# Issuing part of the loads and swaps of a fused attention and feed-forward kernel from GpSimd, and copying w_out in pairs

## The chip, the core and the metric

The kernel runs on one core of a Trainium2 chip. The metric is the device time of one execution in microseconds (us). The core has TensorE (PE; its weight loads are listed as PEld), VectorE (DVE), ScalarE (ACT), GpSimd (POOL) and SyncE (SP), each with an instruction queue of its own that is worked off in order. Data move by DMA on 16 DMA engines; a DMA is an instruction in the queue of the engine that issues it.

## What is computed

Two blocks in a row, all in float32:

```python
# attention: q, k, v are (8, 8, 576, 64); tau = 0.02
scores = scale * np.matmul(q, k.transpose(0, 1, 3, 2))
thresh = np.max(scores, axis=-1, keepdims=True) - tau
scores = np.where(scores >= thresh, scores, -1000000000.0)
scores = scores - np.max(scores, axis=-1, keepdims=True)
attn = np.exp(scores)
attn = attn / (np.sum(attn, axis=-1, keepdims=True) + 1e-09)
x = np.matmul(attn, v)          # then regrouped to (4608, 512)
# feed-forward: w_in (512, 1024), w_out (1024, 512), g_ln (1024)
h = x @ w_in
solu = h * softmax(h)
ln = (solu - mean(solu)) / np.sqrt(var(solu) + 1e-06) * g_ln
out = ln @ w_out
```

The feed-forward weights arrive as 64-bit floats and are taken apart and put together again as 32-bit ones on the chip.

## The kernel before, in words

The attention is cut into 144 **slots**, 18 for each of the 8 batches; a slot is 128 query rows against the 576 keys of two heads. The program is written out by hand as a loop of **rounds**, one per slot and some more at the end; the list of jobs of each round sets the order in every engine's queue. A tile of the feed-forward part (128 tokens) is spread over four rounds and more: two halves of `x @ w_in` (`ff_h`), two halves of `ln @ w_out` (`ff_o`), and the steps between.

One slot goes through the engines like this, with the line of each step:

- PE: `scores`, s_ps (L399). DVE: the row's largest score, nth (L420). ACT: threshold (L435) and exponential with row sums (L444).
- One round later, POOL: `normalise`, which takes the reciprocal of the sums (L451, L452) and multiplies the two tiles w by it (L454, two instructions). DVE: `blocks`, two block transposes T<-w (L466).
- After each second slot, SP: the DMAs wT<-T (L475, L477; L482 for the last slots of a batch), which bring the rows of a block under each other.
- Some three rounds after the slot, PE: attention times v (L507); ACT copies it out (L537).

A feed-forward tile goes PE h_ps (L570), DVE maximum (L585), ACT exponential (L594), DVE product u (L600), POOL L605 and L606, DVE statistics (L615, L616), POOL L619 to L626, ACT V<-u (L636), DVE u (L641, `ff_norm2`), then `ff_swap` (L647): four DMAs of 64 KB that exchange halves of V and u, then DVE transpose uT<-V (L662), PE o_ps (L675), ACT copy ob (L690), SP stores. u, V and uT have one buffer each, so the next tile's ACT exponential (L594) waits until the swap has read u.

The loads. Batch 0 is loaded at the start. For batch 1, q and k come by `load_four` (L135), four DMAs of 144 KB a call, called at the ends of rounds 10 (k), 11 (q), 15 (k) and 16 (q); v comes by `load_v` (L144) at the ends of rounds 17 and 18, and of 24 and 25. For batches 2 to 7, q and k come by `load_natural` (L166), 288 KB each, several rounds ahead of their use, and v by `load_v`, one part a round. All of them are issued by SP. In the program's order each DMA of SP's queue waits for the completion of an earlier DMA of the same queue, as a rule the eighth before it, whose counter it takes over.

In rounds 0 to 15 the 16 pieces of the two weight matrices are converted: DVE L258, L274, L290, L295, ACT L263 and L266, and on POOL one product a round (L305, `weight_c`), which stands in POOL's queue behind that round's `normalise`. The last 8 pieces belong to w_out. Of each of these, one round later, `weight_d` (L308) makes a copy with its two halves of rows exchanged, by two DMAs of 128 KB on SP's queue (L312). `ff_o` starts only when all are issued (`w2_done`).

The order of the jobs at the end of a round: `blocks`, the late jobs of the feed-forward part, the small POOL jobs `scale_natural` (L172) and `gather_ends` (L178), the weight pieces, `weight_d`, and last the loads due in this round:

```python
            if rnd - 1 in pieces:
                weight_d(pieces[rnd - 1])
                w2_done = pieces[rnd - 1] == NW - 1
            for job in load_at.pop(rnd, []):
                job()
```

The swap of a tile is a job of the middle of a round, after that round's `normalise` and `weight_c`.

Of the kernel before, what the change touches and what calls it, by code (L numbers as in the profile page):

```python
# [16 lines left out]
P = 128  # L17
# [3 lines left out]
def kernel(  # L21
# [27 lines left out]
    nc = tc.nc  # L49
# [10 lines left out]
    ROWS = (slice(0, 64), slice(64, P))  # L60
# [10 lines left out]
    w2 = const.tile([P, 2 * NC, DM], F32, name="w2")  # L71
# [60 lines left out]
        whole_rows[i, nm] = raw.rearrange("p (m d) -> p m d", m=NK)  # L132
        (queue or nc.sync).dma_start(out=raw, in_=rows_of[nm][P * i : P * i + P])

    def load_four(i, nm):  # L135
        heads_of = rows_of[nm][P * i : P * i + 2 * P].rearrange("(j e p) n -> e j p n", j=2, e=2)
        for e in range(2):
            tag = "ends" if nm == "q" and i > NP else nm
            raw = loads.tile([P, NK * D], F32, tag=tag, bufs=BUFS[tag], name=nm)
            whole_rows[i, nm, e] = raw.rearrange("p (m d) -> p m d", m=NK)  # L140
            for j in range(2):
                nc.sync.dma_start(out=raw[ROWS[j]], in_=heads_of[e, j])

    def load_v(b, hf, parts):  # L144
        d = halves.setdefault((b, hf), {})
        if 0 in parts:
            d["v"] = loads.tile([P, 4, NK, D], F32, tag="v", bufs=3, name="v")
        to = d["v"].rearrange("p h m d -> p h (m d)")
        rows = rows_of["v"][64 * (H * b + 4 * hf) :][0:256]
        for part in parts:  # L150
            nc.sync.dma_start(**(
                dict(
                    out=to.rearrange("p (e o) n -> p o e n", o=2)[:, 0],
                    in_=rows.rearrange("(e r) n -> r e n", e=2),
                ),
                dict(out=to[:, 1], in_=rows[64:192]),
                dict(out=to[ROWS[1], 3], in_=rows[0:64]),
                dict(out=to[ROWS[0], 3], in_=rows[192:256]),
            )[part])

    qk_rows = {
        nm: x.rearrange("b h (i a t) d -> a (b h i) (t d)", a=2, t=NK)
        for nm, x in (("q", q), ("k", k))
    }

    def load_natural(i, nm, a):  # L166
        natural[i, nm, a] = raw = loads.tile([P, NK * D], F32, tag=nm, bufs=BUFS[nm], name=nm)
        nc.sync.dma_start(out=raw, in_=qk_rows[nm][a, 64 * i : 64 * i + P])

    def scale_natural(i, a):  # L170
        raw = natural[i, "q", a]
# [135 lines left out]

    def weight_d(x):  # L308
        c = x - 2 * NP
        if c >= 0:  # L310
            for r in range(2):
                nc.sync.dma_start(out=w2[ROWS[r], 2 * c + 1], in_=w2[ROWS[1 - r], 2 * c])  # L312

# [268 lines left out]
    def ff_max(t):  # L582
        d = ffn[t]
        d["nm"] = small.tile([P, 1], F32, tag="hm", name="hm")
        nc.vector.tensor_reduce(out=d["nm"], in_=d["h"], axis=AX.X, op=ALU.max, negate=True)  # L585
# [52 lines left out]
    def ff_norm2(t):  # L638
        d = ffn[t]
        rs, nb = d["norm"]  # L640
        nc.vector.tensor_scalar(  # L641
            out=d["u"], in0=d["u"], scalar1=rs, scalar2=nb, op0=ALU.mult, op1=ALU.add
        )

    def ff_swap(t):  # L647
        d = ffn[t]
        for g in range(2):
            for r in range(2):  # L650
                to, of = 64 * r + 32 * g, 64 * r + 32 * (1 - g)
                nc.sync.dma_start(
                    out=d["V"][to : to + 32, 1 - g],
                    in_=d["u"][of : of + 32, DFF // 2 * g : DFF // 2 * g + DFF // 2],
                )
# [72 lines left out]
        ]  # L728

    load_at = {}  # L730
    scale_at, turn_at, ends_at = {}, {}, {}
    for at, hf, what in (
        (17, 0, (0,)),
        (18, 0, (1, 2, 3)),
        (PER + 6, 1, (0,)),
        (PER + 7, 1, (1, 2, 3)),
    ):
        load_at.setdefault(at, []).append(lambda hf=hf, what=what: load_v(1, hf, what))
    for i, at, nm in ((NP, 10, "k"), (NP, 11, "q"), (NP + 2, 15, "k"), (NP + 2, 16, "q")):
        load_at.setdefault(at, []).append(lambda i=i, nm=nm: load_four(i, nm))  # L740
    for i in range(2 * NP):
        ends_at[(9, 10, 11, 12, 21, 23, 26, 28)[i]] = i
    for i in range(2 * NP, NPAIR, 2):
        b, hf = divmod(i // 2, 2)
        ats = ((-5, -3), (-1, 1)) if hf else ((-13, -11), (-9, -7))
        if b == 2:
            ats = ((-3, -2), (-1, 1)) if hf else ((-13, -11), (-9, -5))
        for nm, pieces_at in zip("qk", ats):
            for a, at in enumerate(pieces_at):
                at += PER * b  # L750
                if b == 2:
                    of = at - 3 - (at in (PER + 7, PER + 9))
                else:
                    of = (at - 3) // 4 * 4
                load_at.setdefault(of, []).append(
                    lambda i=i, nm=nm, a=a: load_natural(i, nm, a)
                )
                turn_at[at] = i, nm, a
                if nm == "q":
                    scale_at[at - 1] = i, a  # L760
        for j in range(2):
            ends_at[PER * b + ats[0][1] + 4 + j] = i + j
        if hf:
            v_ats = 3, 5, 5, 7
        elif b == 2:
            v_ats = -9, -7, -5, -3
        else:
            v_ats = (-11, -7, -3, -3) if b % 2 else (-9, -5, -1, -1)
        for part, at in enumerate(v_ats):
            load_at.setdefault(PER * b + at, []).append(  # L770
                lambda b=b, hf=hf, part=part: load_v(b, hf, (part,))
            )

    with tc.manual_schedule():
# [12 lines left out]
        load_pair(3, "q", nc.sync)  # L787
        nc.sync.dma_start(out=g_rows, in_=g_ln.rearrange("(c p) -> c p", p=P))
        weight_load(4, nc.sync)
        load_v(0, 0, (0,))  # L790
        weight_load(5, nc.sync)
        tags, tiles = zip(take("tp"), take("tp"))
        constants(tiles[1][:, 1022:1023])
# [12 lines left out]
        pieces = {r: x for r, x in enumerate(range(1, NW))}  # L806
        whole = {0: 1, 2: 2, 4: 3}
        for r, hf, parts in ((1, 0, (1, 2, 3)), (3, 1, (0,)), (5, 1, (1, 2, 3))):
            load_at[r] = [lambda hf=hf, parts=parts: load_v(0, hf, parts)]

        ready = []
        rnd = 0
# [6 lines left out]
        begin, middle, late, norms = {}, {}, {}, {}  # L819
        while True:  # L820
# [10 lines left out]
            if rnd == NS:  # L831
# [4 lines left out]
                if quarter == 2:  # L836
                    between.append(cur)
                    cur = None
                    quarter = 0
                assert quarter != 3  # L840
            if rnd == 13:
                prev, cur, quarter = cur, None, 0
            if (
# [3 lines left out]
                cur = ready[0][1].pop(0)  # L847
# [60 lines left out]
            if step == ("h", 0):  # L908
                ff_h(cur, 0, rnd + 1 < NS, beside)
                quarter = 1  # L910
            elif step == ("h", 1):
                ff_h(cur, 1, None, beside)
                quarter = 2
                by = rnd + 2 * (rnd == 14)
                late.setdefault(by, []).append(lambda t=cur: (ff_max(t), ff_exp(t)))
                late.setdefault(by + 1, []).append(lambda t=cur: (ff_mul(t), ff_sum(t)))
                middle.setdefault(by + 2, []).append(lambda t=cur: ff_stats(t))
                if rnd + 6 < NS:
                    norms[by + 3] = cur
                else:  # L920
                    late.setdefault(rnd + 2, []).append(lambda t=cur: ff_norm(t))
                middle.setdefault(by + 3, []).append(lambda t=cur: (ff_norm2(t), ff_swap(t)))

                at = by + 4 if more or not ready or len(ready[0][1][0]) == 1 else rnd + 6
                if cur == (0, 1, 1):
                    middle.setdefault(rnd + 6, []).append(lambda t=cur, at=rnd + 6: ff_turn(t, at))
                else:
                    late.setdefault(at, []).append(lambda t=cur, at=at: ff_turn(t, at))
                if not more:
                    between.append(cur)  # L930
                    cur = None
                    quarter = 0
            elif step == ("o", 0):
                if prev is not None:
                    ff_o(prev, 0)
                quarter = 3
            elif step == ("o", 1):
                if prev is not None:
                    ff_o(prev, 1)
                    last = not (more or ready or cur or between)  # L940
                    begin.setdefault(rnd + 1, []).append(lambda t=prev, last=last: ff_out(t, last))
                    late.setdefault(rnd + 1, []).append(lambda t=prev, last=last: ff_store(t, last))
                prev, cur = cur, None
                quarter = 0
            if attending is not None:
# [3 lines left out]
                b, kind, hp = attending  # L949
# [67 lines left out]
```

## Time and profile before

| | before |
|---|---|
| times of three runs, us | 858.46, 858.96, 855.51; median 858.46 |
| time of the profiled execution, us | 855.96 |
| its span, us | 854.2 |
| busy share of the span | PE 96%, DVE 80%, ACT 67%, POOL 58% |
| DMA | 168.5 MB, mean 197 GB/s; the SP queue's packets take 77.3% of the 16 engines' time |
| mean granted TensorE clock | 0.987 |

The span is what lies between the first and the last instruction of the profiled execution; 1.76 us of its time lie outside it. A row of the timeline is start, duration, engine, line, operation, tiles, count, and in brackets how long the engine stood idle before it and who released it. A row of the table by stretches gives, for each engine, busy us and the number of instructions. DMA-issuing instructions are not counted as busy on any engine. No DMA of the kernel before is issued by GpSimd.

### The profile page before, as it was taken

What the parts mean: (1) busy time and instruction counts of PE and PEld (TensorE: products, weight loads), DVE (VectorE), ACT (ScalarE), POOL (GpSimd) and SP (SyncE); (2) the same over time, 40 slices, a digit from 0 to 9 for tenths busy, and PEclk for the clock granted to TensorE, in tenths of its full rate; (3) what the DMA queues carried; (4) which work ended last, traced back from release to release, by engine and by line L of the source; (5) the groups of instructions that cost most, each with busy time, mean ns of one, the idle gap of its engine ahead of it and who ended that gap; (6) DMA issues with size and microseconds to landing.
All of it is one profiled execution on the core that took longest, in us unless ns stands there. A gap on an engine that the chain in (4) does not pass through costs nothing.

```text
span 854.2 us, 36120 instructions
## 1 busy us (share of the span) xinstructions
PE 819.7 (96%) x15363; PEld 613.4 (72%) x15363; DVE 680.4 (80%) x1241; ACT 572.3 (67%) x1127; POOL 499.1 (58%) x945
## 2 busy tenths in 40 slices
PE   6679889999999999999999999999999999999997
PEld 5456666667677787777688877777777777777655
DVE  6999868889788888888788878888888888787361
ACT  6888857877666666666676667766667777775121
POOL 3888637666556656565566666565666655555120
PEclk8889999999999999999999999999999999999999
DMA  9989897898889788887889787888888887655212
GB/s 339 265 236 231 208 206 185 227 250 208 225 208 227 194 191 205 219 214 181 216 212 220 194 177 200 212 212 212 200 207 228 202 195 188 154 136 140 67 39 63
DMA packets 75442, 168.54 MB, mean 197 GB/s; under 512 B 11274, under 2 KB 32786, under 8 KB 75282
## 3 DMA queue, kind: packets, MB, share of 16 engines
q1 hardware_dynamic: 74994, 165.82, 77.3%
q8 instruction: 120, 1.97, 1.0%
q10 hardware_dynamic: 288, 0.43, 0.2%
q14 instruction: 40, 0.33, 0.1%
HBM read 46.14 MB, written 9.44 MB: 65 GB/s over the span
## 4 chain that ended last, share of the span: by engine, by line
PE 80%; DVE 7%; DMA 6%; ACT 3%; issue 2%; POOL 1%; SPq 1%; DVEq 0%; ACTq 0%
PE o_ps L675 27%; PE h_ps L570 21%; PE s_ps L399 15%; PE pv L507 14%; DMA wT<-T 4%; PE h_ps L560 3%; DVE T L466 2%; DVE w L420 2%; ACT w L435 1%; ACT w L444 1%; DVE w L290 1%; DMA V<-u 1%; POOL w L454 0%; PE tp L336 0%; SPq L482 0%
## 5 line engine op out<-in xcount | busy, mean ns | idle before, releaser
L435 ACT ACTIVATE w<-s_ps,nth 128x576 f32<-128x576 f32 x280 | 196.9, 738 | 110.5 <-DVE nth L420 92.0
L675 PE MATMUL o_ps<-w,uT 64*64 64x256 f32 x4608 | 268.4, 376 | 1.3 <-DVE uT L662 0.6
L675 PEld LDWEIGHTS o_ps<-w,uT 64*64 64x64 f32 x4608 | 221.0, 133 | 55.2 <-ACT xh L537 12.0
L420 DVE CUSTOM_DVE_ANT_0 w<-s_ps,tau_t 128x576 f32<-128x576 f32 x280 | 200.1, 751 | 73.7 <-PE s_ps L399 46.3
L454 POOL TENSOR_SCALAR w<-w,sm 128x576 f32<-128x576 f32 x288 | 221.3, 780 | 14.3
L466 DVE STREAM_TRANSPOSE T<-w 128x576 f32<-128x576 f32 x288 | 207.7, 756 | 24.4 <-POOL w L454 23.7
L570 PE MATMUL h_ps<-w,xh 64*64 64x512 f32 x1856 | 220.4, 590 | 0.0
L444 ACT ACTIVATE w<-w,ntau 128x576 f32<-128x576 f32 x288 | 219.5, 766 | 0.0
L507 PEld LDWEIGHTS pv<-wT,v 64*64 64x64 f32 x5760 | 170.4, 135 | 40.7 <-issue 22.9
L399 PE MATMUL s_ps<-kT,qT 64*64 64x64 f32 (+1 forms) x2048 | 173.5, 415 | 16.6 <-ACT w L435 12.5
L507 PE MATMUL pv<-wT,v 64*64 64x128 f32 (+1 forms) x5760 | 173.1, 263 | 7.2 <-DMA wT<-T 5.0
L570 PEld LDWEIGHTS h_ps<-w,xh 64*64 64x64 f32 x1856 | 114.5, 133 | 81.4 <-issue 52.1
L451 POOL TENSOR_SCALAR sm<-sm 128x2 f32<-128x2 f32 x144 | 36.2, 252 | 194.5 <-ACT w L444 191.1
L452 POOL TENSOR_TENSOR sm<-sm,mone 128x2 f32<-128x2 f32 x144 | 108.2, 751 | 12.0
L399 PEld LDWEIGHTS s_ps<-kT,qT 64*64 64x64 f32 x2048 | 70.5, 137 | 25.4 <-ACT w L435 18.0
L537 ACT COPY xh<-pv 128x256 f32<-128x256 f32 x64 | 25.4, 397 | 72.5 <-PE pv L507 72.4
L636 ACT ACTIVATE V<-u,nb,rs 128x1024 f32<-128x1024 f32 x36 | 44.7, 1241 | 41.3 <-POOL nb L626 34.8
L662 DVE STREAM_TRANSPOSE uT<-V 128x1024 f32<-128x1024 f32 x36 | 44.3, 1231 | 21.4 <-DMA V<-u 20.7
L444 ACT ACTIVATION_READ_ACCUMULATOR w<-w,ntau 128x1 f32 x288 | 55.3, 192 | 0.0
L600 DVE TENSOR_TENSOR u<-h_ps,u 128x1024 f32<-128x1024 f32 x36 | 42.8, 1189 | 9.9 <-ACT u L594 9.9
L641 DVE TENSOR_SCALAR u<-u,rs,nb 128x1024 f32<-128x1024 f32 x36 | 34.9, 969 | 17.5 <-ACT V L636 17.4
L594 ACT ACTIVATE u<-h_ps,hm 128x1024 f32<-128x1024 f32 x36 | 40.2, 1117 | 9.9 <-DMA V<-u 5.6
(81 smaller groups left out, 563.7 us busy)
## 6 DMA issues: line engine op xcount, KB each, us to landing
wT<-T SPq DMA_DIRECT2D x160, 288.0 KB, 6.7
wT<-T SPq DMA_DIRECT2D x64, 576.0 KB, 5.5
v<-in_v_dram SPq DMA_DIRECT2D x16, 576.0 KB, 5.7
V<-u SPq DMA_DIRECT2D x144, 64.0 KB, 3.4
out_dram<-ob SPq DMA_DIRECT2D x71, 128.0 KB, 2.6
q<-in_q_dram SPq DMA_DIRECT2D x28, 288.0 KB, 6.0
k<-in_k_dram SPq DMA_DIRECT2D x27, 288.0 KB, 6.5
qT<-flip SPq DMA_DIRECT2D x48, 144.0 KB, 3.5
```

Of the source, the lines that this page charges most:

```text
L399: nc.tensor.matmul(out=ps[h][ROWS[y], ks], lhsT=lhsT, rhs=d["kT"][ROWS[h], ks], start=True, stop=True,)
L420: nc.vector.tensor_tensor_reduce(out=w, in0=ps[:, 0:S], in1=(zero if loose else tau_t).to_broadcast([P, S]), scale=1.0, scalar=BIG, op0=AL ...
L435: nc.scalar.activation(out=d["w"][x], in_=d["w"][x] if d["loose"] else d["ps"][x][:, 0:S], func=AF.Prelu, bias=d["nth"][x], scale=-1.0, al ...
L444: nc.scalar.activation(out=w, in_=w, func=AF.Exp, bias=ntau, scale=1.0, accum_out=sm[:, x : x + 1])
L452: nc.gpsimd.tensor_tensor(out=sm, in0=sm, in1=mone, op=ALU.pow)
L454: nc.gpsimd.tensor_scalar(out=w, in0=w, scalar1=sm[:, x : x + 1], scalar2=1.0, op0=ALU.mult, op1=ALU.mult)
L466: nc.vector.transpose(out=T[:, :, r, h, :], in_=w)
L507: nc.tensor.matmul(out=to, lhsT=d["v"][ROWS[u], (h0 + h - u) % 4, m,], rhs=rhs, start=m == 0, stop=m == NK - 1,)
L570: mm = nc.tensor.matmul(out=h[ROWS[y], f], lhsT=x[ROWS[r], c, ROWS[y]], rhs=w1_parts[ROWS[r], c, part ^ r], start=part == 0 and c == 0, st ...
L636: nc.scalar.activation(out=V, in_=u, func=AF.Identity, bias=nb, scale=rs)
L662: nc.vector.transpose(out=uT, in_=d["V"].rearrange("p y (m x) -> p m y x", x=32))
L675: nc.tensor.matmul(out=d["o"][ROWS[z], 512 * (r ^ other) : 512 * (r ^ other) + 256], lhsT=d["uT"][ROWS[r], m].rearrange("p y x -> p (y x)" ...
```

## The change

Three things are changed. (1) `load_four`, `load_v` and `load_natural` take the queue as an argument; for everything after batch 0 it is GpSimd's. (2) `ff_swap` takes the queue too; for the four ordinary tiles of batch 0 (not for the tile of left-over rows) it is GpSimd's. (3) `weight_d` does nothing for an even piece of w_out and copies two pieces with each of its two DMAs for an odd one. The rounds and the places in the order of jobs are kept.

```diff
-    def load_four(i, nm):
+    def load_four(i, nm, queue):
...
-                nc.sync.dma_start(out=raw[ROWS[j]], in_=heads_of[e, j])
+                queue.dma_start(out=raw[ROWS[j]], in_=heads_of[e, j])
-    def load_v(b, hf, parts):
+    def load_v(b, hf, parts, queue):
...
-            nc.sync.dma_start(**(
+            queue.dma_start(**(
...
-    def load_natural(i, nm, a):
+    def load_natural(i, nm, a, queue):
...
-        nc.sync.dma_start(out=raw, in_=qk_rows[nm][a, 64 * i : 64 * i + P])
+        queue.dma_start(out=raw, in_=qk_rows[nm][a, 64 * i : 64 * i + P])
...
     def weight_d(x):
         c = x - 2 * NP
-        if c >= 0:
+        if c > 0 and c % 2:
+            pair_of = w2.rearrange("p (c two) n -> p two c n", two=2)[:, :, c - 1 : c + 1]
             for r in range(2):
-                nc.sync.dma_start(out=w2[ROWS[r], 2 * c + 1], in_=w2[ROWS[1 - r], 2 * c])
+                nc.sync.dma_start(out=pair_of[ROWS[r], 1], in_=pair_of[ROWS[1 - r], 0])
...
-    def ff_swap(t):
+    def ff_swap(t, queue):
...
-                nc.sync.dma_start(
+                queue.dma_start(
...
+    late_loads = nc.gpsimd
...
-        load_at.setdefault(at, []).append(lambda hf=hf, what=what: load_v(1, hf, what))
+        load_at.setdefault(at, []).append(lambda hf=hf, what=what: load_v(1, hf, what, late_loads))
...
-        load_at.setdefault(at, []).append(lambda i=i, nm=nm: load_four(i, nm))
+        load_at.setdefault(at, []).append(lambda i=i, nm=nm: load_four(i, nm, late_loads))
...
-                    lambda i=i, nm=nm, a=a: load_natural(i, nm, a)
+                    lambda i=i, nm=nm, a=a: load_natural(i, nm, a, late_loads)
...
-                lambda b=b, hf=hf, part=part: load_v(b, hf, (part,))
+                lambda b=b, hf=hf, part=part: load_v(b, hf, (part,), late_loads)
...
-        load_v(0, 0, (0,))
+        load_v(0, 0, (0,), nc.sync)
...
-                middle.setdefault(by + 3, []).append(lambda t=cur: (ff_norm2(t), ff_swap(t)))
+                middle.setdefault(by + 3, []).append(lambda t=cur: (ff_norm2(t), ff_swap(t, nc.gpsimd if t[0] < 1 and len(t) > 1 else nc.sync)))
```

136 DMAs go from SP's queue to GpSimd's: 16 of the swaps (64 KB each), 16 of `load_four` (144 KB), 48 of `load_natural` (288 KB) and 56 of `load_v` (14 of 576 KB, 14 of 288 KB, 28 of 144 KB). The 16 copies of w_out become 8 of twice the size. The queues of PE, DVE and ACT keep their instructions and their order.

More of the change, by code (lines that the diff above doesn't have):

```diff
@@ L808 @@
         for r, hf, parts in ((1, 0, (1, 2, 3)), (3, 1, (0,)), (5, 1, (1, 2, 3))):
-            load_at[r] = [lambda hf=hf, parts=parts: load_v(0, hf, parts)]
+            load_at[r] = [lambda hf=hf, parts=parts: load_v(0, hf, parts, nc.sync)]
         ready = []
```

## The prediction

> **What bounds the kernel now.** I read first the busy shares of the page, then a table by stretches (rounds 10 to 15, 16 to 21, and the long middle).
>
> ```profile
> PE 819.7 (96%) x15363; PEld 613.4 (72%) x15363; DVE 680.4 (80%) x1241; ACT 572.3 (67%) x1127; POOL 499.1 (58%) x945
> ```
>
> ```profile
> 58.00:92.60 34.60, 31.16 (x596) 21.64 (x587) 32.74 (x66) 30.67 (x63) 29.62 (x45) 1.00 0.86 212
> 92.60:127.90 35.30, 31.25 (x722) 24.13 (x720) 26.53 (x51) 23.16 (x50) 17.17 (x34) 1.00 0.86 207
> 160.00:740.00 580.00, 575.69 (x11014) 443.87 (x11010) 482.62 (x876) 405.99 (x804) 353.81 (x686) 1.00 0.83 206
> ```
>
> The columns after the stretch and its length are busy us of PE, PEld, DVE, ACT and POOL, then granted clock, DMA share and GB/s. From 160 to 740 us PE stands idle for 4.3 us of 580: nothing done for other engines there can gain more than that. Before 58 us the queues are unchanged but for the first copies of w_out. So the result is decided in the two stretches from 58 to 128 us, where PE is idle for 3.4 + 4.0 us. In the first DVE is busy for 32.7 of 34.6 us and POOL for 29.6 (86%): this is where the last weight pieces are converted, and where the change puts its first new work on POOL. So the timeline of POOL in rounds 10 and 11 comes next, with the DVE rows that wait for it:
>
> ```profile
> 62.43 1.28 POOL L305 TENSOR_TENSOR w<-w,em 128x512 f32<-128x512 f32 x1
> 63.66 0.44 POOL L178 COPY qe<-qT 128x64 f32<-128x64 f32 x1
> 64.20 0.52 POOL L451 TENSOR_SCALAR sm<-sm 128x2 f32<-128x2 f32 x1
> 64.80 1.01 POOL L452 TENSOR_TENSOR sm<-sm,mone 128x2 f32<-128x2 f32 x1
> 65.91 1.47 POOL L454 TENSOR_SCALAR w<-w,sm 128x576 f32<-128x576 f32 x2
> 67.34 1.28 POOL L305 TENSOR_TENSOR w<-w,third 128x512 f32<-128x512 f32 x1
> 68.56 0.11 POOL L110 MEMSET mark<- 128x1 f32 x1
> 68.59 0.45 POOL L178 COPY qe<-qT 128x64 f32<-128x64 f32 x1
> 69.37 0.29 POOL L451 TENSOR_SCALAR sm<-sm 128x2 f32<-128x2 f32 x1 [0.32 <-ACT w L444]
> ```
>
> ```profile
> 66.18 0.74 DVE L420 CUSTOM_DVE_ANT_0 w<-s_ps,tau_t 128x576 f32<-128x576 f32 x1
> 66.85 1.43 DVE L466 STREAM_TRANSPOSE T<-w 128x576 f32<-128x576 f32 x2
> ```
>
> POOL has no gap here but 0.1 and 0.32 us. The first of the two L454 ends at 65.91 + 0.73 = 66.65; the transpose that reads it starts at 66.85. The slack is 0.2 us.
>
> The waits of the same stretch, and SP's queue, show what the change can cure:
>
> ```profile
> DVE uT L662 <- DMA V<-u: 5.5, 2, 4.9
> PE pv L507 <- DMA wT<-T: 3.3, 4, 1.9
> ```
>
> ```profile
> 69.01 2.52 SPq L142 DMA_DIRECT2D k<-in_k_dram  x4
> 113.91 4.56 SPq L652 DMA_DIRECT2D V<-u  x4
> ```
>
> The swap issued at 113.9 takes SP 4.56 us, behind loads and wT; DVE waits for its landing until 122.4 (4.9 us), and ACT and PE behind it.
>
> **The price of one DMA on POOL** is not in the trace, since POOL issues none. Call it P. From below: the cheapest POOL arithmetic with a wait, L451 on two numbers a row, takes 0.25 us on average; from above: L305, 1.28 us. On SP one of the four k loads takes 2.52 / 4 = 0.63 us. I take P = 0.75 us, the mean of L452 (751 ns), POOL's row for a short program whose time does not come from data, and near SP's 0.63. [...]
>
> **Part 1, loads of rounds 10 and 11 (8 DMAs).** Four k loads come behind L178 at 63.66, ahead of L451 at 64.20, so this slot's normalising ends 4P - 0.1 later, and the transpose, after its 0.2 us of slack, 4P - 0.3 later. Behind it on DVE stand the weight steps and the next slot's maxima (L420), for these ACT's L435, for that PE's scores two rounds on; DVE has no gap before 91 us to catch up in. Four q loads follow behind the L178 of 68.59; there POOL has 0.32 us of idle time, so 4P - 0.3 more. Together 8P - 0.6 = 5.4 us, all on the path.
>
> **Part 2, the swaps and the loads of rounds 15 to 27.** In round 15, behind L305 (ends 91.65), come the four swaps and four k loads, ahead of the L451 that starts at 92.59 after 0.95 us of idle time; the transpose of that slot already waits for POOL (0.46 us), so it has no slack: 8P - 0.95 = 5.05 us. The four q loads of round 16 meet 1.96 us of POOL's idle time and 1.2 us of slack ahead of the transpose at 100.21: hidden up to P = 0.8, beyond that 4P - 3.2. The four v loads of rounds 17 and 18 and the four swaps of round 19 meet idle times of 1.89 and 3.83 us and 2.1 us of slack: nothing. The third tile's swaps come behind the L454 that ends at 141.07, with a v load behind them, and POOL has no idle time there before 144.5: 5P = 3.75 us, of which the next transpose (144.93) has 1.16 us of slack and DVE 0.76 + 0.43 us of idle time after it: 5P - 2.35 = 1.4 us. The fourth's (162.5) meet 1.66 us of idle time and more at 166: nothing. The swaps wait for u (L641), which in round 15 is done at 89.81, before POOL gets there.
>
> **Part 3, what SP gives back.** 36 early DMAs and 8 of the copies leave SP. What can vanish on PE: the two waits of pv for wT at 93 and 94 us (0.62 + 0.46), the wait for uT at 97.97 (0.58), and PE's idle time from 114.1 to 127.9, 13.80 - 11.74 = 2.06 us, which follows the late swap. Together 3.7 us. The paired copies: the last pair is issued in the same round as before (95 us). Its 256 KB may land later than 128 KB did (4.6 us in the median); the second half of o_ps that reads it starts at 102.42, so nothing, at most 1 us.
>
> **Part 4, the long middle.** At most 136 - 16 - 16 = 104 DMAs fall there, 78 us of POOL at P = 0.75, against 580 - 354 = 226 us in which it is idle; the pairs of `load_natural` stand ahead of idle times of some 2.2 us (2 x 0.75 = 1.5). Cost nothing; the cover is gone from P = 226 / 104 = 2.2 us. SP's relief gains little: PE's waits for wT there are 1.1 us in all.
>
> **Sum.** 5.4 + 5.05 + 1.4 - 3.7 = +8.2 us, made against the profiled execution: 855.96 + 8.2 = 864.2. That execution lies 2.5 us below the median of the three runs; the four times have the mean 857.2, and I predict on that level: **865 us**. With P = 0.25: 1.4 + 1.05 - 3.7 = -1.2; with P = 1.28: 9.6 + 9.3 + 1.9 + 4.05 - 3.7 = +21.2.
>
> **Rivals.**
> 1. *POOL's DMAs are cheap and SP was the brake: faster.* With P = 0.25 the cost is 2.45 us; if freeing SP removes the whole of PE's idle time in the second stretch and the middle (4.05 + 4.3), the result is -5.9: 851. For it: SP issues without a gap from 86 to 125 us, and the 4.9 us wait. Against it: PE's idle time is spread over many small waits for ACT and DVE. It decides at P below about 0.3.
> 2. *The two cancel.* At P = 0.4: 2.6 + 2.25 - 3.7 = +1.1: 858. The change then does nothing measurable.
> 3. *DVE and POOL lock each other out: slower by more.* In the trace DVE's L258 takes 0.42 us alone and 0.73 to 0.80 us where it starts beside POOL's L305 (63.20, 68.21), and L641 0.81 or 1.20 us. If such waits also hold up POOL's issuing, P goes to the upper end, 1.28: 857.2 + 21.2 = 878. [...]
> 4. *The loads share the DMA engines (86% busy) from a second queue and delay wT* is part of the range only: wT lands after 6.7 us now, and a swap or load that no longer stands in front of it takes as much away as it adds.
>
> That the change doesn't do what it says is excluded by the order of instructions: 136 DMAs stand in POOL's queue, and PE, DVE and ACT keep theirs.
>
> **Chances.** The forecast (P from 0.5 to 1.1): 0.40; rival 1: 0.30; rival 2: 0.20; rival 3: 0.10. Half a per cent (4.3 us) is about what a measurement of this kernel can tell from no change. Faster by more than that 0.30 (rival 1), within it 0.20, slower 0.50 (forecast and rival 3). The range of 8 in 10 reaches from 850 (rival 1 with a us to spare) to 878 (P at its upper end); the forecast's own is 860 to 872.
>
> **What would show it.** Right: POOL's DMA instructions of 0.6 to 0.9 us each; the L451 that starts at 64.20 now starts some 3 us later; DVE's transposes at 66.85, 71.80 and 94.48 wait for POOL (the total of "DVE T <- POOL w", 2.3 us from 60 to 130, rises to about 10); PE's idle time from 58 to 93 us rises from 3.4 to about 9; the wait for V<-u (4.9 us) goes. Wrong: POOL's DMAs at 0.3 us or less, or the transposes unmoved; or a long middle that is longer than 580 us for the same rounds, which would mean that POOL has become its bound.

## The result, and the profile after

The changed kernel takes 879.92 us (median of six runs, 874.95 to 884.59), the kernel before 858.99 (six runs, 855.51 to 862.62): a ratio of 1.0244, with a 95% interval from 1.0207 to 1.0280. The forecast was 865, in a range of 850 to 878. The sign was right and the size was not: +21 us in place of +8. The profiled execution took 881.67 us, its span is 879.8. A ratio compares undisturbed runs only, so it can differ a little from the quotient of the medians of all runs.

The lines of the page that answer to those of before (busy time of the engines, then the DMA queues: packets, MB, share of the 16 engines):

```profile
PE 827.4 (94%) x15363; PEld 611.7 (70%) x15363; DVE 678.7 (77%) x1241; ACT 571.9 (65%) x1127; POOL 577.7 (66%) x1081
...
q1 hardware_dynamic: 57842, 131.73, 58.4%
q0 software_dynamic: 9600, 34.09, 14.3%
```

POOL has 136 more instructions. Its DMAs form a queue of their own, q0, with 3.55 KB a packet (34.09 MB / 9600) where SP's q1 has 2.28: 7168 of its packets have 4608 bytes, and 14,336 of 2304 bytes are gone from SP's queue (16,256 before, 1920 now). The table by stretches, in the columns of before:

```profile
58.00:92.60 34.60, 30.38 (x548) 19.32 (x548) 31.35 (x64) 27.94 (x54) 31.01 (x50) 1.00 0.77 186
92.60:127.90 35.30, 29.54 (x606) 21.63 (x602) 23.55 (x45) 23.39 (x52) 30.94 (x56) 0.95 0.79 209
160.00:740.00 580.00, 563.79 (x10720) 428.46 (x10716) 467.75 (x854) 392.14 (x781) 399.26 (x762) 0.99 0.78 202
```

From 160 to 740 us PE is idle for 16.2 us, where it was 4.3: the stretch in which I had put no cost at all. To compare the same work and not the same clock time, take the starts of the rows of DVE's maximum (L420 before, L421 after; slot 0 is the first). After minus before is +0.6 us at slot 8, +8.1 at slot 20, +6.0 at 24, +8.3 at 40, and then +13.7 at slot 44, +17.0 at 60, +21.6 at 96 and +25.2 at 140. So in this execution what the forecast speaks of is over by slot 40, in its forecast size, and the long middle, slots 24 to 140, takes 19.3 us more.

**The early stretch.** POOL's rows of rounds 10 and 11, in answer to those of before (start, duration, engine, line, operation):

```profile
64.28 0.44 POOL L178 COPY qe<-qT 128x64 f32<-128x64 f32 x1
64.66 2.33 POOL L142 DMA_DIRECT2D k<-in_k_dram  x4
67.06 0.23 POOL L452 TENSOR_SCALAR sm<-sm 128x2 f32<-128x2 f32 x1
67.38 0.72 POOL L453 TENSOR_TENSOR sm<-sm,mone 128x2 f32<-128x2 f32 x1
68.21 1.46 POOL L455 TENSOR_SCALAR w<-w,sm 128x576 f32<-128x576 f32 x2
```

```profile
68.99 1.50 DVE L467 STREAM_TRANSPOSE T<-w 128x576 f32<-128x576 f32 x2 [1.44 <-POOL w L455]
```

The four k loads stand where they were expected, and the transpose behind them waits 1.44 us. Round 15, where the four swaps and four k loads come together, on POOL, DVE and PE:

```profile
95.29 2.12 POOL L653 DMA_DIRECT2D V<-u  x4
97.40 2.06 POOL L142 DMA_DIRECT2D k<-in_k_dram  x4
99.53 0.23 POOL L452 TENSOR_SCALAR sm<-sm 128x2 f32<-128x2 f32 x1
```

```profile
101.44 1.50 DVE L467 STREAM_TRANSPOSE T<-w 128x576 f32<-128x576 f32 x2 [3.71 <-POOL w L455]
```

```profile
104.21 3.26 PE L676 MATMUL o_ps<-w,uT 64*64 64x256 f32 x28 [3.04 <-DVE uT L663]
```

Read upwards: PE waits 3.04 us for uT, uT stands on DVE behind the transpose T, and T waits 3.71 us for POOL. That is part 2 of the forecast, as told there.

**The middle.** One feed-forward tile, at the same work, before and after. Before, SP alone:

```profile
542.20 0.57 SPq L475 DMA_DIRECT2D wT<-T  x1
542.81 2.73 SPq L477 DMA_DIRECT2D wT<-T  x2
545.64 3.91 SPq L652 DMA_DIRECT2D V<-u  x4
549.60 1.40 SPq L703 DMA_DIRECT2D out_dram<-ob  x2
551.09 1.22 SPq L188 DMA_DIRECT2D kT<-flip  x2
552.35 0.61 SPq L151 DMA_DIRECT2D v<-in_v_dram  x1
```

The v load stands behind the swap, the stores and kT. The transpose uT<-V starts at 551.32, before that load is issued, and waits for nothing. After, SP and POOL, and then DVE and PE:

```profile
564.70 2.88 SPq L478 DMA_DIRECT2D wT<-T  x2
567.67 3.44 SPq L653 DMA_DIRECT2D V<-u  x4
571.16 1.40 SPq L704 DMA_DIRECT2D out_dram<-ob  x2
```

```profile
567.86 0.81 POOL L151 DMA_DIRECT2D v<-in_v_dram  x1
```

```profile
576.18 1.25 DVE L663 STREAM_TRANSPOSE uT<-V 128x1024 f32<-128x1024 f32 x1 [3.36 <-DMA V<-u]
```

```profile
577.57 2.77 PE L676 MATMUL o_ps<-w,uT 64*64 64x256 f32 x45 [0.84 <-DVE uT L663]
```

POOL issues the load 0.19 us after SP began with the swap. The load's bytes now move beside the swap's: from 570 to 576 us q0 takes 60.9% of the 16 engines' time and q1 36.1%, and the 128 packets of the swap start from 570.28 to 575.08, over 4.8 us, where they took 2.9 before (547.67 to 550.57). uT starts 8.5 us after the swap's issue (576.18 - 567.67), where it was 5.7 (551.32 - 545.64), and PE waits. DVE's wait for V<-u over the whole run, before and after (total, times, longest):

```profile
DVE uT L662 <- DMA V<-u: 20.7, 17, 4.9
```

```profile
DVE uT L663 <- DMA V<-u: 52.4, 26, 5.3
```

What PE waits for from slot 24 to slot 140, before (137 to 765 us) and after (143 to 790 us; total, times, longest):

```profile
PE s_ps L399 <- issue: 2.4, 2, 1.3
PE pv L507 <- DMA wT<-T: 1.1, 2, 0.8
PE pv L507 <- ACT w L444: 0.3, 1, 0.3
```

```profile
PE o_ps L676 <- DVE uT L663: 4.4, 6, 1.8
PE o_ps L676 <- issue: 4.1, 2, 3.8
PE s_ps L400 <- issue: 4.0, 2, 2.9
PE s_ps L400 <- DVE both L421: 1.5, 3, 0.9
PE pv L508 <- DMA wT<-T: 1.4, 2, 0.9
PE s_ps L400 <- ACT w L436: 1.0, 2, 0.7
```

3.8 us have become 16.4. The waits for uT are the swap's. The rows "<- issue", in which PE waits for nothing that the profile shows, rise from 2.4 to 8.1 us. I read them as PE out of instructions. The three longest come within the first six slots of batches 2, 4 and 5, two of them at the places of the two waits of before. In the two longest a 16 KB packet of the instruction queue begins only after PE has stopped (at 238.35 and 527.83 us; in the two of before it begins 1.2 and 2.0 us ahead of the stop). Such a packet ends 1.2 to 1.7 us before PE goes on in every one of the 56 waits of this kind of half a microsecond or more that the profiles of all kernels of this document show after 128 us (1.26 to 1.51 us in the five of the two kernels compared here), so I take the fetch for what these waits end with. The longest, and two slices of the table by stretches around it (PE's clock is the third figure from the end):

```profile
241.05 1.44 PE L676 MATMUL o_ps<-w,uT 64*64 64x256 f32 x9 [3.79 <-issue]
```

```profile
236.00:240.00 4.00, 1.25 (x22) 0.71 (x14) 2.79 (x4) 2.00 (x5) 2.65 (x6) 1.00 0.94 194
240.00:244.00 4.00, 2.95 (x28) 2.10 (x31) 0.00 (x0) 0.00 (x0) 0.70 (x1) 0.60 0.41 104
```

The DMA engines are 94% busy in the 4 us in which PE stops, and in the 4 us after them the granted clock is 0.60. The record of the clock has three spells of 3.41 us at half speed between 60 us and the end of the work, at 104, 241 and 531 us, here at the end of PE waits of about 3 us (3.04, 3.79, 2.94); the profile of before has none between 58 and 852 us. Each takes up to 1.7 us of PE's work (half of 3.41, an estimate). The three begin whole multiples of 3.413 us apart (136.53 and 290.13 us, 40 and 85 times), and in the step of 3.41 us ahead of each PE was idle for 3.04, 3.41 and 2.77 us in all; from 58 us to the last 9 us no other step of that grid in this profile has more than 1.82. In the profiles of all kernels of this document the spells begin on such a grid, and each of the 28 between 61 us and the last 9 us follows a step in which PE was idle for 1.55 us or more in all; of the other steps at full speed none has more than 1.89 us of idle time. The waits and two of the spells make 16.4 - 3.8 + 2 x 1.7 = 16.0 us of the 19.3 by which these slots became longer.

### The profile page after: what moved, and what is told of

Same layout as the page of the kernel before. It is cut to its first block, busy times and chain, and to the rows that moved or that the text cites. A ratio compares the mean times of both kernels' runs of the same rounds, so it can differ in the third digit from the quotient of the medians.

```text
span 879.8 us, 36167 instructions
## 1 busy us (share of the span) xinstructions
PE 827.4 (94%) x15363; PEld 611.7 (70%) x15363; DVE 678.7 (77%) x1241; ACT 571.9 (65%) x1127; POOL 577.7 (66%) x1081
## 3 DMA queue, kind: packets, MB, share of 16 engines
q0 software_dynamic: 9600, 34.09, 14.3%
## 4 chain that ended last, share of the span: by engine, by line
PE 58%; DVE 13%; POOL 9%; DMA 8%; issue 6%; ACT 3%; SPq 2%; DVEq 0%; ACTq 0%; POOLq 0%
PE o_ps L676 21%; PE h_ps L571 14%; PE pv L508 10%; PE s_ps L400 10%; DMA V<-u 5%; DVE w L421 3%; PE h_ps L561 3%; DVE T L467 3%; DMA wT<-T 2%; POOL w L455 2%; DVE bs L616 2%; POOL sm L453 2%; SPq L653 2%; ACT w L436 1%; ACT w L445 1%
## 5 line engine op out<-in xcount | busy, mean ns | idle before, releaser
L676 PE MATMUL o_ps<-w,uT 64*64 64x256 f32 x4608 | 271.5, 380 | 12.3 <-DVE uT L663 7.5
L676 PEld LDWEIGHTS o_ps<-w,uT 64*64 64x64 f32 x4608 | 229.3, 134 | 65.8 <-issue 28.7
L421 DVE CUSTOM_DVE_ANT_0 w<-s_ps,tau_t 128x576 f32<-128x576 f32 x280 | 199.4, 748 | 53.4 <-PE s_ps L400 43.6
L508 PEld LDWEIGHTS pv<-wT,v 64*64 64x64 f32 x5760 | 168.1, 135 | 39.6 <-issue 27.5
L400 PE MATMUL s_ps<-kT,qT 64*64 64x64 f32 (+1 forms) x2048 | 172.7, 416 | 21.6 <-ACT w L436 15.2
L508 PE MATMUL pv<-wT,v 64*64 64x128 f32 (+1 forms) x5760 | 170.2, 261 | 5.2 <-DMA wT<-T 4.0
L571 PEld LDWEIGHTS h_ps<-w,xh 64*64 64x64 f32 x1856 | 108.9, 133 | 88.9 <-issue 66.2
L452 POOL TENSOR_SCALAR sm<-sm 128x2 f32<-128x2 f32 x144 | 36.9, 256 | 111.5 <-ACT w L445 106.1
L606 POOL TENSOR_SCALAR se<-se 128x1 f32<-128x1 f32 x36 | 8.4, 233 | 71.2 <-ACT u L595 70.8
```

The source lines that it names most:

```text
L400: nc.tensor.matmul(out=ps[h][ROWS[y], ks], lhsT=lhsT, rhs=d["kT"][ROWS[h], ks], start=True, stop=True,)
L421: nc.vector.tensor_tensor_reduce(out=w, in0=ps[:, 0:S], in1=(zero if loose else tau_t).to_broadcast([P, S]), scale=1.0, scalar=BIG, op0=AL ...
L508: nc.tensor.matmul(out=to, lhsT=d["v"][ROWS[u], (h0 + h - u) % 4, m,], rhs=rhs, start=m == 0, stop=m == NK - 1,)
L571: mm = nc.tensor.matmul(out=h[ROWS[y], f], lhsT=x[ROWS[r], c, ROWS[y]], rhs=w1_parts[ROWS[r], c, part ^ r], start=part == 0 and c == 0, st ...
L676: nc.tensor.matmul(out=d["o"][ROWS[z], 512 * (r ^ other) : 512 * (r ^ other) + 256], lhsT=d["uT"][ROWS[r], m].rearrange("p y x -> p (y x)" ...
```

## The experiments

Theory A: the late loads (batches 2 to 7) cost by sharing the DMA engines with SP's urgent transfers from a queue of their own; the loads of batch 1 cost POOL's time. Theory B: it is POOL's time everywhere. A third: the late start of the middle has an after-effect. All runs stand beside runs of the kernel before on the same chip (medians 856.8 to 858.6 us). The number of late loads is 96; where an expectation says 104, I had counted wrongly.

**One part at a time.** Each of four kernels keeps one part of the change and has the rest as before:

```diff
 e1  ff_swap(t, nc.gpsimd if t[0] < 1 and len(t) > 1 else nc.sync)    all loads nc.sync, single copies
 e2  load_four(i, nm, nc.gpsimd), load_v(1, hf, what, nc.gpsimd)      late loads and swaps nc.sync, single copies
 e3  load_natural(i, nm, a, nc.gpsimd), load_v(b, hf, (part,), nc.gpsimd)   batch 1 and swaps nc.sync, single copies
 e4  weight_d in pairs                                                all loads and swaps nc.sync
```

> Only the 16 swaps of batch 0 go to GpSimd; all loads stay on SP and w_out is copied piece by piece. Theory A (most of the loss comes from the late loads, which on a queue of their own run at the same time as wT and the swaps, and the rest from GpSimd's time in rounds 10 to 19): GpSimd is late by 4 x 0.53 us at each swap, of which its idle times hide most, and the swap of the second tile lands earlier: -2 to +2 us against before. Theory B (GpSimd's time is what costs, everywhere): four swaps of 2.1 us each, +2 to +4 us.

> Only the loads of batch 1 (the 16 half loads of rounds 10, 11, 15, 16 and 8 of v) go to GpSimd. Both theories: rounds 10 and 11 cost 8 x 0.57 - 0.6 = 4 us at most, as the changed kernel's trace shows (+3.1 us at slot 13), rounds 15 and 16 about 2 us more, no swap in front of them: +4 to +6 us.

> Only the loads of batches 2 to 7 (96 DMAs) go to GpSimd. In the changed kernel the slots from 41 to the end lose 17 us against before. Theory A and theory B both say +14 to +18 us here; a third theory, that the losses of the middle are an after-effect of the late start (a shifted order of arrival), says under +5 us.

> Only the paired copies of w_out. Both theories: no wait in the changed kernel is put down to them: within 1 us of before. If the later landing of the first copy of a pair held up o_ps: +1 to +3 us.

| part alone | median, us | ratio | interval |
|---|---|---|---|
| e1, swaps | 859.82 | 1.0005 | 0.9966 to 1.0043 |
| e2, loads of batch 1 | 861.57 | 1.0022 | 0.9985 to 1.0059 |
| e3, late loads | 874.02 | 1.0124 | 1.0043 to 1.0204 |
| e4, pairs | 857.21 | 0.9971 | 0.9939 to 1.0002 |

Only the late loads are clearly slower. The parts add up to less than the whole, 1.2% against 2.4%. e3 has only four runs: at the upper end of its interval the sum is 2.0%, and with the intervals of the other parts it reaches the whole. e2 is not clear of 1, so what batch 1's loads cost by themselves is not shown by its time.

**POOL's time without the loads, the loads without POOL's time, other rounds, all loads.**

```diff
 e5  load_natural(i, nm, a, nc.sync); spend(1)     load_v(b, hf, (part,), nc.sync); spend(1)
+    def spend(n):
+        for _ in range(n):
+            nc.gpsimd.tensor_tensor(out=idle_w, in0=mone[:, 0:1], in1=mone[:, 0:1], op=ALU.pow)
 e6  load_natural(i, nm, a, nc.scalar)             load_v(b, hf, (part,), nc.scalar)
 e7  load_at.setdefault(of + 1, [])                load_at.setdefault(PER * b + at + 1, [])
 e8  all loads from batch 1 on nc.gpsimd; swaps and copies as before
```

> The late loads (batches 2 to 7) stay on SP's queue as before; in their places POOL does a power of one number a row (0.57 us in the profile, beside 0.53 to 0.65 us for a load's issue), 104 times: POOL's time without the second queue. Theory A (loads on a queue of their own run beside the swap and the copies wT, which land later; what it costs is DMA time, not POOL's): within 2 us of before, and the wait of uT for V<-u stays near 21 us in all. Theory B (what it costs is POOL's time, 104 x 0.6 = 60 us, which delays the normalising of the slots): the median rises by 10 to 15 us, as in the run with the late loads alone (874.0), and the wait of T for POOL's w rises from 24 to 27 us or more, with PE stalls behind it.

> The late loads are issued by ACT: a queue of their own, and no time of POOL's. Theory A: the wait of uT for V<-u rises from 21 to 40 us or more, and the median by 8 to 15 us. Theory B: POOL has nothing more to do, so no rise from that; ACT, idle for a third of the time, takes 104 x 0.6 us more, which by B's reasoning costs at most 4 us, and the wait of uT for V<-u stays near 21 us.

> The late loads on POOL as in the changed kernel, but each one round (5.4 us) later, so that none is issued in the round in which SP issues the swap. Theory A: the wait of uT for V<-u falls from 49 us back to 20 to 28, and the median lies within 5 us of before. Theory B: POOL issues as much as before the shift, so the median stays 10 to 15 us above before.

> All 120 loads from batch 1 on are issued by POOL, the swaps and the copies of w_out stay as before. The two parts alone measured +2.9 us (loads of batch 1) and +15.4 us (later loads, four runs with a wide interval). If the parts add up (the whole change is then these two, with swaps and pairs giving little): 875 to 878. If the early and the late loads make each other worse: 881 or more. If the swaps on POOL are needed for the full loss: below 874.

| | median, us | ratio | interval | uT waits for V<-u, us |
|---|---|---|---|---|
| e5, powers on POOL | 855.88 | 0.9979 | 0.9957 to 1.0001 | 17.2 |
| e6, late loads on ACT | 874.10 | 1.0189 | 1.0156 to 1.0222 | 20.1 |
| e7, late loads on POOL, a round later | 872.31 | 1.0177 | 1.0135 to 1.0219 | 39.7 |
| e8, all loads on POOL | 875.77 | 1.0233 | 1.0200 to 1.0266 | 51.1 |

e5 ends theory B for the middle: the same time of POOL costs nothing there. e8 is the whole change within the intervals, so the swaps and the pairs add nothing that can be measured; whether early and late loads make each other worse stays open, since e3's interval is too wide for it. e6 came out with A's time, but not with A's sign: the wait for V<-u did not move. Its profile shows why: beside 21 of the 25 swaps from 200 to 780 us ACT's queue moved less than 120 KB up to uT, so the loads were hardly ever beside the swap. Its time has other causes: ACT itself stands idle ahead of a load (3.62 us up to 570.06, with a v load issued at 569.54), and PE's wait for ACT ahead of the scores rises from 12.5 to 18.5 us; what the second queue costs alone can't be taken from it. e7 was badly aimed: it moved some v loads out of the swap's round and others to just before it, and PE's wait for wT from slot 24 to 140 is 9.7 us there (1.1 before, 1.4 in the changed kernel), so a round later the loads seem to meet wT instead. But it has swaps of both kinds in one run. A swap with a v load issued 2.4 us ahead (SP, POOL, DVE), and one of the same run without (SP, DVE):

```profile
534.12 3.54 SPq L652 DMA_DIRECT2D V<-u  x4
```

```profile
531.73 0.82 POOL L151 DMA_DIRECT2D v<-in_v_dram  x1
```

```profile
544.29 1.25 DVE L662 STREAM_TRANSPOSE uT<-V 128x1024 f32<-128x1024 f32 x1 [4.49 <-DMA V<-u]
```

```profile
582.24 3.56 SPq L652 DMA_DIRECT2D V<-u  x4
```

```profile
587.65 1.25 DVE L662 STREAM_TRANSPOSE uT<-V 128x1024 f32<-128x1024 f32 x1
```

10.2 us against 5.4 from the swap's issue to uT. Over all swaps from 200 to 780 us of this profile: with 660 to 1010 KB of POOL's queue moved in between 7.7 to 10.2 us (six swaps), with less than 60 KB 5.4 to 7.6 (ten), with amounts between these 5.4 to 7.7 (nine). In the record a load's packet of 4608 bytes on POOL's queue occupies an engine for 0.18 us in the median, a packet of 2048 bytes on SP's queue, the swap's size, for 0.12 (changed kernel and e3 alike). In the changed kernel's tile shown above, the 60.9% of the engines' time that went to POOL's queue, beside 36.1% for SP's, go with 8.5 us from issue to uT against 5.7 before; here it is 10.2 against 5.4 us. How an engine chooses between the two queues is not shown.

**Which loads, and the queue without the bytes.** e9 adds, to all loads on SP, small DMAs on POOL; e10 and e11 put only the late v, only the late q and k on POOL; e12 only the loads of batch 2, with the pairs.

```diff
 e9      for _ in range(n):
+            nc.gpsimd.dma_start(out=idle_w, in_=qk_rows["q"][0, 0:P, 0:32])
 e10 load_natural(i, nm, a, nc.sync)          load_v(b, hf, (part,), nc.gpsimd)
 e11 load_natural(i, nm, a, nc.gpsimd)        load_v(b, hf, (part,), nc.sync)
 e12 load_natural(i, nm, a, nc.gpsimd if i < 3 * NP else nc.sync), load_v: nc.gpsimd if b < 3
```

> The late loads stay on SP's queue as before; at each of their 104 places POOL also issues a DMA of 128 rows of 128 bytes (16 KB) into a tile that nobody reads: POOL's issue and its queue, but hardly any bytes. If the loss comes from the loads' bytes running beside SP's urgent transfers (theory A): within 2 us of before (855 to 860). If it comes from issuing DMAs on POOL as such (a DMA issue holds POOL or others up in a way that the power of the run before, which cost nothing, did not): 868 to 875, as with the late loads themselves.

> Only the late loads of v are issued by POOL, those of q and k stay on SP. In the changed kernel the late v loads are issued in the same rounds as the swap, those of q and k one round after it. Theory A in its narrow form (it is the swap beside the load that counts): most of the 15 us, 866 to 873, and the wait of uT for V<-u above 40 us. A wider form (any load from a second queue delays whatever SP sends at that time): about half, 862 to 867.

> Only the late loads of q and k are issued by POOL, those of v stay on SP. Narrow form of A (swap and v load): within 4 us of before, the wait of uT for V<-u below 30 us. Wider form: about half of the 15 us, 862 to 867.

> The paired copies of w_out, and of all loads only those of batch 2 on POOL. In the run with all late loads on POOL the slots 20 to 30 began up to 2.2 us earlier than before, while SP's queue was full there; the loss came later. If that gain stays and the later loss goes: 1 to 4 us faster than before. If the loads of batch 2 cost as much as those of a later batch (15 / 6 = 2.5 us): no gain, 856 to 861.

| | median, us | ratio | interval | uT waits for V<-u, us |
|---|---|---|---|---|
| e9, small DMAs, one tile | 916.66 | 1.0684 | 1.0641 to 1.0727 | 22.3 |
| e10, late v | 867.98 | 1.0130 | 1.0103 to 1.0156 | 57.1 |
| e11, late q and k | 862.91 | 1.0045 | 1.0020 to 1.0070 | 19.1 |
| e12, batch 2, pairs | 859.36 | 1.0025 | 1.0004 to 1.0045 | 17.8 |

e9 has a flaw of its own. Its small DMAs all write one tile, so each waits for the landing of the one before, and POOL stands still meanwhile; its waits say so:

```profile
POOL idle_w L170 <- DMA idle_w<-in_q_dram: 129.3, 53, 6.6
```

It says nothing of the question, but it shows what a wait at the head of POOL's queue costs: 129 us of it made the kernel 59 us slower. e10 and e11 move the same bytes (14.2 MB each), and v, most of it in the swap's round, costs more than twice as much as q and k; only v brings the wait for V<-u. e10 came out as the narrow form of theory A has it. e11 has the wait of the narrow form and a time in the range of the wide one, so q and k cost something that isn't the swap. e12: the gain that late loads off SP's queue seemed to bring around slot 24 isn't there.

**Mended runs.**

```diff
 e13 of = PER * b + at                        # v; q and k as in e3
+    load_at.setdefault(of + (of % 4 == 3), [])
 e14 load_four(i, nm, nc.sync); spend(4)      load_v(1, hf, what, nc.sync); spend(len(what))
 e15 nc.gpsimd.dma_start(out=idle_w[next(turn_of) % 8], in_=qk_rows["q"][0, 0:P, 0:8])
 e16 as e4
```

> As the run with the late loads on POOL (874.0), with one thing moved: the v loads that were due in the round in which SP issues the swap (24 of the 48, all those of rounds that leave 3 when divided by 4) come one round later; all else keeps its round. In the run with every late load shifted, a swap with no load from POOL beside it had its transpose 5.4 to 7.6 us after its issue, one with 660 to 1000 KB beside it 7.7 to 10.2 us; the shift had moved other v loads in front of the swap. Theory A, narrow form: the wait of uT for V<-u falls from 49 us to below 28, and the median to 860 to 865, the level of the late q and k loads alone (862.9). If the swap is not what counts: 870 or more, whatever the wait does.

> All loads on SP as before; in the places of batch 1's loads (rounds 10, 11, 15 to 18, 24, 25) POOL does as many powers of one number a row, 0.57 us each: POOL's time alone, in the stretch where my forecast put its cost. By its own sums with P = 0.57 and no swaps: rounds 10 and 11 8 x 0.57 - 0.6 = 4.0, round 15 4 x 0.57 - 0.95 = 1.3, together +5.3 us and no relief of SP: 861 to 864. If the early loads cost by their bytes as the later ones do: within 2 us of before.

> The run with small extra DMAs on POOL once more, without its flaw: there each wrote the same tile, so that POOL stood and waited for the landing of its own last DMA (129 us in all). Now they write eight tiles in turn (128 rows of 32 bytes), so POOL issues and goes on. POOL's issue and queue without the bytes: within 2 us of before (855 to 860) if the bytes are the cause; 868 or more if issuing on POOL is.

> The paired copies of w_out alone once more, for a narrower interval (0.9971, from 0.9939 to 1.0002, before): the one part that may be worth keeping. 854 to 858, 0 to 4 us faster than before.

| | median, us | ratio | interval |
|---|---|---|---|
| e13, late loads, v clear of the swap | 867.21 | 1.0132 | 1.0109 to 1.0154 |
| e14, powers in place of batch 1's loads | 859.77 | 1.0036 | 1.0020 to 1.0052 |
| e15, small DMAs, eight tiles | 859.40 | 1.0024 | 0.9995 to 1.0052 |
| e16, pairs | 857.59 | 1.0010 | 0.9983 to 1.0036 |

e15: issuing 96 DMAs on POOL costs at most half a per cent, so it is the bytes. e14: in the early stretch POOL's time does cost, 3 us where the forecast's sums gave 5.3; it lies between the two outcomes that were named for it. e16: the pairs change nothing that can be measured. e13 is half a hit. The group of uT in its page is that of before again:

```profile
L662 DVE STREAM_TRANSPOSE uT<-V 128x1024 f32<-128x1024 f32 x36 | 44.3, 1231 | 21.6 <-DMA V<-u 21.4
```

and PE no longer waits for uT from slot 24 to 140. But the median fell to 867.2 only, not to 860 to 865, and the ratio (1.0132) is not below e3's (1.0124, with its wide interval): by the times alone a gain is not shown. What PE still waits for there is mostly instructions:

```profile
PE s_ps L399 <- issue: 3.4, 2, 2.2
PE pv L507 <- DMA wT<-T: 2.5, 3, 1.5
PE o_ps L675 <- issue: 2.3, 2, 1.9
```

**The two halves of that rest.**

```diff
 e17 e13 with load_natural(i, nm, a, nc.sync)
 e18 e13 with
-    of = (at - 3) // 4 * 4
+    of = (at - 3) // 4 * 4 + ((at - 3) % 4 > 1)
```

> Only the late v loads on POOL, and those of the swap's rounds one round later; q and k stay on SP. The run with the v loads in their old rounds was 868.0, the wait of uT for V<-u 57 us, and PE stood 6.4 us for uT from the 24th to the 140th slot. If the v loads cost only by their place beside the swap: 856 to 860, uT's wait 18 to 25 us, PE's wait for uT gone. If every load from a second queue costs, wherever it stands: 862 or more.

> As the run with the v loads moved clear of the swap (867.2), and of the two q and k loads that are issued together every fourth round (batches 3 to 7) the second one round later. In that run PE stood for 5.7 us without instructions (rows '<- issue') from the 24th to the 140th slot against 2.4 before, at the rounds in which two loads are issued together, with an instruction fetch just before PE went on. If two loads together hold up PE's instruction fetch: these rows fall to 3.5 us or less and the median to 860 to 864. If the fetches are late for another reason: 865 to 869, rows as before.

e17: 860.99 us, ratio 1.0038 (1.0012 to 1.0064). Against e10 only the round of 34 of the 48 v loads differs (the expectation of e13 counts 24), and 7 of its 11 us are gone; uT waits 20.5 us for V<-u, not 57.1. It ended one microsecond above what was expected: v loads clear of the swap are cheap, not free. e18: 865.59 us, ratio 1.0087 (1.0055 to 1.0120). The rows of missing instructions fell as expected, from 5.7 to 2.4 us:

```profile
PE pv L507 <- DMA wT<-T: 1.9, 2, 1.6
PE s_ps L399 <- issue: 1.6, 2, 0.8
PE o_ps L675 <- issue: 0.8, 1, 0.8
```

but the median fell by 1.6 us, not by 3 to 7. In its profile the slots from 36 to 140 take only 0.6 us longer than before, and the loss lies between slots 8 and 32 (+8 us), with half-speed spells of PE's clock at 63, 131 and 182 us. No version is clearly faster than the kernel before.

**The middle across the profiles.** From slot 24 to slot 140 the kernels that leave the late loads on SP repeat within 2.1 us, one execution each, so this stretch is a finer measure than the whole time. All figures are in us; e9 is left out for its flaw, e6 and e7 because most of PE's waiting there is for others (ACT and wT):

| late loads on a second queue | slots 24 to 140 | PE waits for uT | PE waits "<- issue" |
|---|---|---|---|
| none (before, e1, e2, e4, e5, e14, e15, e16) | 625.8 to 627.9 | 0 | 1.3 to 3.2 |
| e12, batch 2's only | 628.8 | 0 | 0.7 |
| e17, v clear of the swap | 629.3 | 0 | 3.3 |
| e11, q and k | 631.0 | 0 | 5.7 |
| e18, all, v clear, q and k spread | 631.5 | 0 | 2.4 |
| e13, all, v clear | 634.9 | 0 | 5.7 |
| e10, v beside the swap | 639.4 | 6.4 | 3.0 |
| e3, all | 639.7 | 3.0 | 6.3 |
| e8, all, and batch 1's | 641.0 | 3.3 | 6.4 |
| changed kernel, all | 646.4 | 4.4 | 8.1 |

Each wait is there where its loads are and gone where they are moved: the wait for uT comes with v beside the swap, the wait for instructions with q and k issued in pairs.

## Why the forecast was right, and where it was wrong

**What bounds the kernel.** "Nothing done for other engines there can gain more than" 4.3 us in the middle: right, and e4, e5 and e16 gained nothing. The sentence bounds gains only, and I read it as if it bounded losses too.

**The price P.** 0.75 us was too high. POOL's DMAs took 0.50 to 0.82 us, with medians of 0.54 for the pieces of 64 rows and 0.63 for those of 128. L452, from which I took it, is no fixed price of a short program either: a power took 0.57 us on one number a row (L623) and 0.75 on two (L452). With P = 0.55 my sums give 3.8 + 3.45 + 0.4 - 3.7 = +4.0 in place of +8.2.

**Parts 1 and 2** were right in mechanism: rounds 10, 11 and 15 are late by POOL, T's wait for POOL from 60 to 130 us rose from 2.3 to 8.2 us (forecast "about 10"), and powers in place of batch 1's loads cost 3 us. The transpose of round 15 waited 3.71 us, 3.25 more than before; the eight DMAs took 2.12 + 2.06 us, and 4.18 - 0.95 gives 3.2. Not in the sum: the PE wait of 3.04 us that follows ends in 3.4 us at half clock. "PE's idle time from 58 to 93 us rises from 3.4 to about 9" failed (4.2), though slot 13, inside this stretch, is already 3.1 us later than slot 8: PE counts as busy there for nearly as long with fewer instructions done (548, before 596), so idle time was the wrong sign to look for.

**Part 3.** The 4.9 us wait for V<-u went, as said (from 60 to 130 us 1.8 us are left of 5.5). What this was worth, or the pairs, can't be told from nothing: e1 and e16 are within their intervals of 1. That the profiled execution stands at +8.3 us at slot 40, the forecast's size, is luck in part: a smaller P and a clock spell make up for each other, and one execution says little here. The profiled execution of e4, in which POOL issues no DMA, stands at +5.7 us at slot 40.

**Part 4 is the step that failed**: "Cost nothing; the cover is gone from P = 2.2 us". The cover was there: 96 powers or 96 small DMAs in the loads' places cost nothing that matters (0.9979, 1.0024). But the price of a moved DMA isn't only its issue. In SP's queue a load stood behind the swap and its bytes came after it (issued at 552.35, the swap at 545.64). In POOL's queue it starts when POOL gets there, beside the swap (567.86 and 567.67). I had named the sharing as the fourth rival, with wT as what it delays, and dismissed it: "a swap or load that no longer stands in front of it takes as much away as it adds". For wT in this kernel that came out (6.7 us to landing before, 6.5 after; e7, with its wait of 9.7 us, shows that it need not). For the swap it did not (3.4 and 4.4 us): the bytes are the same, but the urgent ones no longer go first. The longer middle stands in the prediction as a sign that "POOL has become its bound"; it came, and by e5 POOL was not the bound. The late loads cost 1.2 to 1.8% by e3, e10 and e11, of the whole 2.4%. Of the v loads' 11 us 7 are shown to be the swap (e10 against e17). That PE's waits "<- issue" end soon after an instruction fetch is shown by the packets (1.2 to 1.7 us, 56 of 56), and that these waits come with the paired q and k loads by e11, e13 and e18; that a fetch starts late because the DMA engines are full is argued.

**Rivals 1 and 2** fell with the size of the late part. **Rival 3**, 878, named nearly the right time for the wrong reason: that DVE holds up POOL's DMAs is not seen (none took over 0.82 us).

**Open**: why e18 keeps 7 us when both causes are gone from its waits in the middle (batch 2's loads, issued in rounds 20 to 34, were not spread); how much of a run's loss is the clock, whose spells fall differently in the profiles (none from 58 to 852 us before; 104, 241 and 531 us in the changed kernel; 63, 131 and 182 us in e18); what e6 would be without ACT's own waits; and whether early and late loads add up.

## What to carry to other kernels

In this kernel a transfer's place in SP's queue was a priority: with the load behind the swap uT started 5.7 us after the swap's issue, with the load beside it on POOL's queue 8.5. Before you move loads to another engine's queue, list the urgent transfers of the same microseconds that they stood behind, and price each of these at the time that it takes beside the load (in e7 7.7 to 10.2 us with 660 to 1010 KB beside the swap, 5.4 to 7.6 with less than 60). POOL's idle time covered the issuing (e15, 1.0024), not the bytes (e3, 1.0124); and if a second queue must be, put its loads in rounds in which the first sends nothing that an engine waits for (860.99 us in e17, 867.98 in e10).

## What the runs showed of the hardware

- PE's waits "<- issue" were up to 3.79 us long in the changed kernel, the longest at a DMA share of 94% (236 to 240 us), where the longest from slot 24 to 140 before was 1.3. PE went on 1.2 to 1.7 us after the end of a 16 KB packet of the instruction queue (56 of 56 such waits of half a microsecond or more, all kernels).
- In 28 of 28 spells of 3.41 us at half clock (all kernels, from 61 us to the last 9 us) PE was idle for 1.55 us or more in the 3.41 us ahead; no other such step at full speed had more than 1.89 us of idle time. In the changed kernel it was 3.04, 3.41 and 2.77 us ahead of the three spells, and at most 1.82 elsewhere.
- POOL took 0.54 us in the median to issue a load of 64 rows, 0.63 for 128 rows and 0.81 for 256 (changed kernel), and the bytes of a row made no difference to speak of: 128 rows of 128 bytes (e9) took 0.60 in the mean, 128 rows of 2304 bytes 0.61.
